# Turning the third weight of the second network in 32 by 32 blocks on VectorE, with four-way loads and a reordered sum

## The chip, the cores and the metric

The kernel runs on one core of one Trainium2 chip. The metric is the time of one execution in microseconds on the device, the median over several runs. Engines are named as in the profile: PE is TensorE (PEld its weight loads), DVE is VectorE, ACT is ScalarE, POOL is GpSimd, SP the engine that here only issues DMAs.

## The reference

Inputs and weights arrive as float64 and are converted on the chip. In short:

```python
attn = concat([a @ state, a2 @ x])       # both softmaxes of x.state^T, 8 batches x 8 heads, 512 + 32 rows, D = 64
x = attn.transpose(0, 2, 1, 3).reshape(8 * 544, 512)
h = np.maximum(x @ w_in, 0.0)            # w_in 512 x 2048   first network
x = h * h @ w_out                        # w_out 2048 x 512
a = x @ w1                               # 512 x 1024        second network
b = x @ w2
h = a * b @ w3                           # w3 1024 x 1024    "third weight"
return h @ w_out2                        # w_out2 1024 x 512
```

No nonlinearity stands between `w3` and the second network's `w_out`, which the kernel calls `w_out2`. The kernel multiplies these two weights with each other once.

## The kernel before

The batches are called c = 0 to 7, with a short ninth group of rows behind them. For each c the first network runs over f = 0 to 15: `h_tile(c, f)` makes 128 of the 2048 hidden columns with six matmuls (L456, tiles `ph`), ACT takes relu and square (L442, L444), and the result is split into a high and a low part of fp32r (`split`: a cast on ACT, L84, and a subtraction on DVE, L85; tile `ghl`). `y_tile(c, f)` follows two tiles behind and adds that slice times `w_out` to the four output banks with twelve matmuls (L494, three passes over high and low parts, `PASSES`). The weight `sw` that `h_tile` reads holds the product of a group of four f with the state: eight small matmuls (L426, `ps_sw`), split again by a cast and a subtraction.

Between these tiles lies the attention of the next batch. `load_xb` loads x in 16 small transfers (L247), `turn_x` turns it in 32 by 32 blocks on DVE (L257, tiles `xT`), eight small matmuls make the scores (L295, `ps_s`), ACT copies them out (L301, tiles `S`), and DVE and ACT do the softmax (L306 to L340). `ps_s`, `ps_sw` and a few others share one PSUM tag, `bank_m`, with two buffers, so `ps_sw` can be written only when ACT has copied the scores out.

Also between the tiles, about one piece for every second tile, the weights of the second network are converted from float64 ("later" pieces 0 to 39: `w_out2`, then 16 of `w3`, then `w1` and `w2`). `load_later` loads one piece of 128 partitions x 512 numbers in a 512 KB transfer (tag `raw`, three buffers, which the x transfers share). `exponents` and `convert64` turn it into float32 with five DVE instructions (L128, L146, L149, L152, L155) and one on ACT (L129). `make_later` stores it from tile `cw` to a scratch in DRAM (L214). All loads and stores are issued by SP, in order.

When the first network ends, w3 comes back from the scratch (`load_stage`, L641, tiles `wst`, a row block kk of 128 x 1024 each). `w3_xpose(kk)` turns it on PE with eight transposes of 128 x 128 (L692, two halves of four, into `bank_m`), and splits each half from PSUM into `w3T`. `w34_rows(kk)` multiplies it with `w_out2` in 24 matmuls (L707). There are eight row blocks. The transposes of the next block stand ahead of the matmuls of this one. Then the second network's products (`quad`, L822, and `out_tile`, L903) run to the end.

The order of instructions on each engine is not the order of the program: the framework's scheduler places instructions of the parts that run beside each other, with gates between some tiles. A change in one part can therefore move the others on every queue. The functions touched, and what calls them:

Of the kernel before, what the change touches and what calls it, by code (L numbers as in the profile page):

```python
# [8 lines left out]
F32 = mybir.dt.float32  # L9
F32R = mybir.dt.float32r  # L10
# [10 lines left out]
def kernel(  # L21
# [37 lines left out]
    def f32(ap):  # L59
        return ap.bitcast(F32)  # L60
# [10 lines left out]
    def bank_m(name):  # L71
        return psum.tile([P, 512], F32, tag="m", bufs=2, name=name)
# [7 lines left out]
    def split(hi, lo, src, hi_on_vector=False):  # L80
        if hi_on_vector:
            nc.vector.tensor_copy(hi, src)
        else:
            nc.scalar.copy(hi, src)  # L84
        return nc.vector.tensor_tensor(out=lo, in0=src, in1=f32(hi), op=ALU.subtract)  # L85
# [20 lines left out]
    def raw_tile(early, name="raw"):  # L106

        if early:
            return wpool.tile([P, 512, 2], I32, tag="wo", bufs=NF, name=name)
        return att.tile([P, 512, 2], I32, tag="raw", bufs=3, name=name)  # L110

    def load64(key, src, early=False):

        t = raw_tile(early)
        flat = t.rearrange("p a b -> p (a b)")
        if isinstance(src, list):
            n = 1024 // len(src)
            for i, a in enumerate(src):
                nc.sync.dma_start(flat[:, i * n:(i + 1) * n], a.bitcast(I32))
        else:  # L120
            nc.sync.dma_start(flat, src.bitcast(I32))
        raws[key] = t
# [9 lines left out]
    def convert64(key, out):  # L132


        t = raws.pop(key)
        hw, lw = t[:, :, 1], t[:, :, 0].bitcast(U32)
        if len(out.shape) == 3:
            n = out.shape[2]
            hw, lw = (v.rearrange("p (k n) -> p k n", n=n) for v in (hw, lw))
        if key not in exps:  # L140
            exponents(key, t)
        e = exps.pop(key)
        m = att.tile([P, 512], I32, tag="cm", bufs=1, name="cm")
        if len(out.shape) == 3:
            e, m = (v.rearrange("p (k n) -> p k n", n=n) for v in (e, m))
        nc.vector.tensor_scalar(  # L146
            out=m, in0=hw, scalar1=0xFFFFF, scalar2=0x100000, op0=ALU.bitwise_and, op1=ALU.bitwise_or
        )
        nc.vector.scalar_tensor_tensor(  # L149
            out=f32(m), in0=lw, scalar=2.0**-32, in1=m, op0=ALU.mult, op1=ALU.add  # L150
        )
        nc.vector.scalar_tensor_tensor(  # L152
            out=e, in0=hw, scalar=-(2**31), in1=e, op0=ALU.bitwise_and, op1=ALU.bitwise_or
        )
        nc.vector.scalar_tensor_tensor(  # L155
            out=out, in0=f32(m), scalar=2.0**-20, in1=f32(e), op0=ALU.mult, op1=ALU.mult
        )

    def load_win(fg, k):
        load64(("win", fg, k), w_in[k * P:(k + 1) * P, fg * 512:(fg + 1) * 512])  # L160
# [33 lines left out]

        open_splits.append(halves)

    w3_s = [dram.tile([P, 2, 512], F32, name=f"w3s{i}") for i in range(N1)]
    w12_s = [[dram.tile([P, 2, 512], F32, name=f"w12s{i}_{k}") for k in range(ND)] for i in range(2)]
    wo2_s = [dram.tile([P, 2, 512], F32, name=f"wo2s{i}") for i in range(N1 // 2)]
    later = [(wo2_s[j // 2][:, j % 2, :], w_out2[j * P:(j + 1) * P, :]) for j in range(N1)]  # L200
    for src, dst in ((w3, w3_s), (w1, w12_s[0]), (w2, w12_s[1])):
        later += [
            (dst[k][:, h, :], src[k * P:(k + 1) * P, h * 512:(h + 1) * 512])
            for k in range(src.shape[0] // P) for h in range(2)
        ]

    def load_later(i):
        if i < len(later):
            load64(("later", i), later[i][1])

    def make_later(i):
        w = att.tile([P, 512], F32, tag="cw", bufs=1, name="cw")
        convert64(("later", i), w)
        nc.sync.dma_start(later[i][0], w)  # L214

    stT = att.tile([P, B, HG, NS], F32, name="stT")
    x9T = pa.tile([P, ND, NT9], F32, tag="x9", name="x9T")
# [421 lines left out]
    def load_stage(key, src):  # L639
        t = w34p.tile([P, 2, 512], F32, tag="wst2", bufs=4, name="wst2")  # L640
        nc.sync.dma_start(t, src)  # L641
        stage[key] = t

    def load_wo2(i):
        load_stage(("wo2", i), wo2_s[i])

    def split_wo2(j):
        t = w34p.tile([P, 2, DM], F32R, tag="wo2", bufs=N1, name="wo2")
# [1 line left out]
        wo2_t[j] = t  # L650

    def load_w3(kk):
        load_stage(("w3", kk), w3_s[kk])

    order = [(c, f) for f0 in (0, 4) for c in range(2) for f in range(f0, f0 + 4)]
    order += [(2, f) for f in range(8)] + [(c, f) for c in range(3) for f in range(8, NF)]
# [28 lines left out]

    w3T = {}

    def w3_xpose(kk):
        for half in range(2):
            ps = bank_m("ps_w3")  # L690
            for j in range(4):
                nc.tensor.transpose(  # L692
                    ps[:, j * P:(j + 1) * P], stage["w3", kk][:, half, j * P:(j + 1) * P], ident
                )
            t = pa.tile([P, 2, 512], F32R, tag=f"sw{half}", bufs=2, name="w3T")
            split(t[:, HI], t[:, LO], ps)
            w3T[kk, half] = t

    w34_t = {}
    w34_s = [dram.tile([P, 2, 2, DM], F32, name=f"w34s{i}") for i in range(N1 // 4)]  # L700
# [221 lines left out]


    rows = list(range(N1 // 2, N1)) + list(range(N1 // 2))
    w3_xpose(rows[0])
    while pend:
        y_tile(*pend.pop(0))
    raw = load_w(0)
    for i, kk in enumerate(rows):
        if i + 1 < N1:  # L930
            w3_xpose(rows[i + 1])
        if i + 4 < N1:
            load_w3(rows[i + 4])
        w34_rows(kk)
        if i == 3:
            make_w(raw)
# [71 lines left out]
```

## Time and profile before

| | us |
|---|---|
| median of 3 runs | 1257.79 |
| the 3 runs | 1257.40, 1257.79, 1259.08 |
| profiled execution | 1257.84 |
| its span | 1256.1 |

Mean granted clock of PE over the span: 0.999 of full speed. 1.74 us of the profiled execution lie outside its span. The page of the profile gives the busy time of each engine, the chain of waits that ended last, and groups of instructions by line. The timeline of an engine gives when each group of equal instructions started and for how long it was busy, with the idle time before it; since matmuls are pipelined, the next one starts before the last one has ended, and the distance of two starts is what a matmul costs on PE.

### The profile page before, as it was taken

Reading aid. Unit: us, or ns where it says so; the run is one execution under the profiler, and the core shown is the slowest. Engines: PE = TensorE matmul, PEld = TensorE weight load, DVE = VectorE, ACT = ScalarE, POOL = GpSimd, SP = SyncE. Lnnn points to the kernel's source line nnn. Section 1 sums busy time; section 2 is a strip of 40 time slices with the busy share of each in tenths; the row PEclk is TensorE's granted clock in tenths of the full one; section 3 lists DMA queues with packets and bytes.
Section 4 is the critical chain, followed back from the end, with each engine's and each line's share of the span. In section 5 each row is a group of like instructions: output and inputs, shape, how many; then the busy total and the mean of one; then the engine's idle time right before and its main releaser. Section 6 shows DMA issues by size and latency. Waiting matters only on the chain.

```text
span 1256.1 us, 17499 instructions
## 1 busy us (share of the span) xinstructions
PE 1235.1 (98%) x6672; PEld 982.1 (78%) x6672; DVE 789.0 (63%) x1403; ACT 659.3 (52%) x1188; POOL 33.5 (3%) x30
## 2 busy tenths in 40 slices
PE   6999999999999999999999999999999999999998
PEld 4667777777777777777799888888888888887886
DVE  6998778677585867742435835555655647474753
ACT  5687768666575756645655434444443524242430
POOL 0000000000000000000000000001500010000000
PEclk9999999999999999999999999999999999999999
DMA  6264646462634535201313520313430521423213
GB/s 218 69 207 145 173 129 201 113 184 82 156 130 86 190 76 173 89 18 34 134 42 111 201 76 9 120 48 126 143 134 9 201 76 52 149 74 128 76 59 117
DMA packets 125268, 143.23 MB, mean 114 GB/s; under 512 B 71680, under 2 KB 75264, under 8 KB 124672
## 3 DMA queue, kind: packets, MB, share of 16 engines
q1 hardware_dynamic: 125184, 142.11, 36.5%
q8 instruction: 52, 0.85, 0.3%
q14 instruction: 32, 0.26, 0.1%
HBM read 96.47 MB, written 45.61 MB: 113 GB/s over the span
## 4 chain that ended last, share of the span: by engine, by line
PE 93%; DMA 2%; ACT 2%; DVE 2%; issue 1%; SPq 0%; ACTq 0%; DVEq 0%
PE y L494 29%; PE po L903 14%; PE qa L822 10%; PE qd L822 7%; PE qc L822 3%; PE ps_w L707 3%; PE qe L822 3%; PE ps_sw L426 3%; PE ab L877 2%; DMA x<-in_x_dram 1%; PE ps_w L692 1%; PE ps_a L364 1%; PE ps_r L372 0%; PE ps_s L295 0%; DMA out_dram<-o 0%
## 5 line engine op out<-in xcount | busy, mean ns | idle before, releaser
L494 PE MATMUL y<-ghl,wo 128*128 128x512 f32 (+1 forms) x1728 | 403.0, 381 | 0.6 <-ACT wo L84 0.5
L494 PEld LDWEIGHTS y<-ghl,wo 128*128 128x128 f32 x1728 | 309.1, 188 | 88.4 <-ACT r L442 12.6
L85 DVE TENSOR_TENSOR ghl<-r,ghl 128x512 fp32r<-128x512 f32 (+1 forms) x144 | 95.0, 660 | 170.1 <-ACT ghl L84 167.4
L822 PE MATMUL qa<-yq,wq 128*128 128x512 f32 x576 | 146.3, 390 | 1.4 <-ACT s L830 1.4
L830 ACT COPY s<-qa 128x512 f32<-128x512 f32 x96 | 56.2, 589 | 143.7 <-PE qa L822 131.2
L822 PEld LDWEIGHTS qa<-yq,wq 128*128 128x128 f32 x576 | 107.5, 188 | 25.5 <-ACT s L830 2.4
L822 PE MATMUL qd<-yq,wq 128*128 128x512 f32 x384 | 98.4, 390 | 0.0
L903 PE MATMUL po<-w34b,c 128*128 128x512 f32 x408 | 95.8, 391 | 0.3 <-DVE o L912 0.3
L903 PE MATMUL po<-w,c 128*128 128x512 f32 x408 | 95.5, 391 | 0.0
L903 PEld LDWEIGHTS po<-w34b,c 128*128 128x128 f32 x408 | 75.7, 188 | 18.0 <-DVE c L85 1.0
L903 PEld LDWEIGHTS po<-w,c 128*128 128x128 f32 x408 | 75.5, 188 | 17.7 <-ACT o L909 1.1
L444 ACT ACTIVATE r<-r 128x512 f32<-128x512 f32 (+1 forms) x144 | 87.5, 608 | 2.9
L84 ACT CAST ghl<-r 128x512 fp32r<-128x512 f32 (+1 forms) x144 | 86.0, 597 | 3.5
L822 PEld LDWEIGHTS qd<-yq,wq 128*128 128x128 f32 x384 | 71.8, 188 | 15.7 <-ACT s L830 0.9
L129 ACT ACTIVATE ce<-ce,ebias 128x512 int32<-128x512 int32 x72 | 52.3, 727 | 44.3 <-DVE ce L128 44.3
L834 DVE TENSOR_TENSOR s<-qa,s 128x512 f32<-128x512 f32 x32 | 22.1, 692 | 75.0 <-ACT s L830 75.0
L780 POOL TENSOR_TENSOR yraw<-yraw,yp 128x512 f32<-128x512 f32 x24 | 32.8, 1373 | 987.9 <-DMA yraw<-yscr 815.2
L84 ACT CAST c<-s 128x512 fp32r<-128x512 f32 x64 | 39.7, 622 | 37.1 <-DVE s L851 36.1
L84 ACT CAST yq<-yraw 128x512 fp32r<-128x512 f32 x70 | 42.6, 622 | 24.1 <-DVE yraw L797 15.5
L912 DVE TENSOR_TENSOR o<-po,opart 128x512 f32<-128x512 f32 x34 | 23.3, 689 | 47.1 <-PE po L903 37.6
L152 DVE SCALAR_TENSOR_TENSOR ce<-raw,ce 128x512 int32<-128x512 int32 x72 | 49.3, 685 | 1.7 <-ACT ce L129 1.7
L85 DVE TENSOR_TENSOR yq<-yraw,yq 128x512 fp32r<-128x512 f32 x70 | 46.8, 684 | 5.0 <-ACT yq L84 4.7
(551 smaller groups left out, 1806.6 us busy)
## 6 DMA issues: line engine op xcount, KB each, us to landing
raw<-in_moe_w_dram SPq DMA_DIRECT2D x32, 512.0 KB, 4.3
yraw<-yscr SPq DMA_DIRECT2D x56, 256.0 KB, 5.5
yscr<-yo SPq DMA_DIRECT2D x52, 256.0 KB, 2.6
raw<-in_moe_w_out_dram SPq DMA_DIRECT2D x24, 512.0 KB, 3.9
oscr<-o SPq DMA_DIRECT2D x34, 256.0 KB, 2.2
opart<-oscr SPq DMA_DIRECT2D x34, 256.0 KB, 2.9
out_dram<-o SPq DMA_DIRECT2D x32, 256.0 KB, 2.9
raw<-in_moe_w_in_dram SPq DMA_DIRECT2D x12, 512.0 KB, 3.9
```

What stands on the lines that cost most here:

```text
L84: nc.scalar.copy(hi, src)
L85: return nc.vector.tensor_tensor(out=lo, in0=src, in1=f32(hi), op=ALU.subtract)
L129: nc.scalar.activation(e, e, ACTF.Relu, bias=ebias, scale=8.0)
L152: nc.vector.scalar_tensor_tensor(out=e, in0=hw, scalar=-(2**31), in1=e, op0=ALU.bitwise_and, op1=ALU.bitwise_or)
L426: mm = nc.tensor.matmul(pss[r][k * NS:(k + 1) * NS, cols], stT[rows, b, k, :], win_t[fg][rows, k, cols], start=True, stop=True, tile_posit ...
L444: nc.scalar.activation(r[:, :n], r[:, :n], ACTF.Square)
L494: nc.tensor.matmul(y_ps[c, d][:, :n], wo_t[f][:, wi, d * P:(d + 1) * P], t[:, gi, :n], start=(f == f0 and k == 0), stop=(f == f1 - 1 and k ...
L707: nc.tensor.matmul(ps, t[:, wi, (j % 4) * P:(j % 4 + 1) * P], wo2_t[j][:, vi, :], start=(j == 0 and k == 0), stop=(j == N1 - 1 and k == 2),)
L780: nc.gpsimd.tensor_tensor(out=t[:, n], in0=t[:, n], in1=p, op=ALU.add)
L822: nc.tensor.matmul(ps, W[w, kt][:, wi, m * P:(m + 1) * P], Y[v, kt][:, vi, :], start=(first and kt == 0 and k == 0), stop=(last and kt == ...
L830: nc.scalar.copy(t, ps)
L903: nc.tensor.matmul(ps, v[:, vi, t * P:(t + 1) * P], w[:, wi, :], start=(m == 0 and k == 0), stop=(m == QM - 1 and k == 2),)
```

## The change

The 16 pieces of w3 get another shape and another way. A piece is now 64 rows x 1024 columns. It is loaded by four transfers: each brings 256 columns of the 64 rows to one quarter (32) of the partitions. The conversion ends in the tile `cm` in place of `cw`, and one DVE instruction turns its 128 x 512 numbers in 32 by 32 blocks into `cw`, which is stored. The scratch is one DRAM tile. When it is read back, block by block, partition 32a+q of the part with number k holds column 256a+32k+q of w3, so the sum over w3's columns runs in another order, and `w_out2` is loaded in that order too, by four transfers of 32 partitions in place of one. The eight transposes on PE per row block are gone; the split reads the loaded tile in SBUF through a view whose innermost run is 32 numbers. Number and shapes of the product's matmuls (L707, now L729) stay as they are.

```diff
--- before.py
+++ after.py
@@ -134,14 +134,14 @@
 
         t = raws.pop(key)
         hw, lw = t[:, :, 1], t[:, :, 0].bitcast(U32)
-        if len(out.shape) == 3:
+        if out is not None and len(out.shape) == 3:
             n = out.shape[2]
             hw, lw = (v.rearrange("p (k n) -> p k n", n=n) for v in (hw, lw))
         if key not in exps:
             exponents(key, t)
         e = exps.pop(key)
         m = att.tile([P, 512], I32, tag="cm", bufs=1, name="cm")
-        if len(out.shape) == 3:
+        if out is not None and len(out.shape) == 3:
             e, m = (v.rearrange("p (k n) -> p k n", n=n) for v in (e, m))
         nc.vector.tensor_scalar(
             out=m, in0=hw, scalar1=0xFFFFF, scalar2=0x100000, op0=ALU.bitwise_and, op1=ALU.bitwise_or
@@ -153,8 +153,9 @@
             out=e, in0=hw, scalar=-(2**31), in1=e, op0=ALU.bitwise_and, op1=ALU.bitwise_or
         )
         nc.vector.scalar_tensor_tensor(
-            out=out, in0=f32(m), scalar=2.0**-20, in1=f32(e), op0=ALU.mult, op1=ALU.mult
+            out=f32(m) if out is None else out, in0=f32(m), scalar=2.0**-20, in1=f32(e), op0=ALU.mult, op1=ALU.mult
         )
+        return f32(m)
 
     def load_win(fg, k):
         load64(("win", fg, k), w_in[k * P:(k + 1) * P, fg * 512:(fg + 1) * 512])
@@ -194,24 +195,46 @@
 
         open_splits.append(halves)
 
-    w3_s = [dram.tile([P, 2, 512], F32, name=f"w3s{i}") for i in range(N1)]
+    w3_s = dram.tile([P, 4 * N1, 256], F32, name="w3s")
     w12_s = [[dram.tile([P, 2, 512], F32, name=f"w12s{i}_{k}") for k in range(ND)] for i in range(2)]
-    wo2_s = [dram.tile([P, 2, 512], F32, name=f"wo2s{i}") for i in range(N1 // 2)]
-    later = [(wo2_s[j // 2][:, j % 2, :], w_out2[j * P:(j + 1) * P, :]) for j in range(N1)]
-    for src, dst in ((w3, w3_s), (w1, w12_s[0]), (w2, w12_s[1])):
+    wo2_s = dram.tile([D1, DM], F32, name="wo2s")
+    later = [(wo2_s[j * P:(j + 1) * P, :], w_out2[j * P:(j + 1) * P, :]) for j in range(N1)]
+    w3_v = w3.rearrange("(i d q) (a c) -> i a q d c", d=2, q=NS, a=4)
+    later += [(w3_s[:, 2 * i:2 * i + 2], [w3_v[i, a] for a in range(4)]) for i in range(2 * N1)]
+    for src, dst in ((w1, w12_s[0]), (w2, w12_s[1])):
         later += [
             (dst[k][:, h, :], src[k * P:(k + 1) * P, h * 512:(h + 1) * 512])
             for k in range(src.shape[0] // P) for h in range(2)
         ]
 
+    turned = range(N1, N1 + 2 * N1)
+
     def load_later(i):
-        if i < len(later):
+        if i >= len(later):
+            return
+        if i >= turned.stop:
             load64(("later", i), later[i][1])
+            return
+        t = raw_tile(False)
+        flat = t.rearrange("p a b -> p (a b)")
+        if i in turned:
+            for q, a in enumerate(later[i][1]):
+                nc.sync.dma_start(
+                    flat[q * NS:(q + 1) * NS].rearrange("p (d c) -> p d c", d=2), a.bitcast(I32)
+                )
+        else:
+            nc.sync.dma_start(flat, later[i][1].bitcast(I32))
+        raws["later", i] = t
 
     def make_later(i):
-        w = att.tile([P, 512], F32, tag="cw", bufs=1, name="cw")
-        convert64(("later", i), w)
-        nc.sync.dma_start(later[i][0], w)
+        if i in turned:
+            m = convert64(("later", i), None)
+            w = att.tile([P, 512], F32, tag="cw", bufs=1, name="cw")
+            nc.vector.transpose(out=w, in_=m)
+        else:
+            w = att.tile([P, 512], F32, tag="cw", bufs=1, name="cw")
+            convert64(("later", i), w)
+        nc.sync.dma_start(later[i][0], w.rearrange("p (d c) -> p d c", d=2) if i in turned else w)
 
     stT = att.tile([P, B, HG, NS], F32, name="stT")
     x9T = pa.tile([P, ND, NT9], F32, tag="x9", name="x9T")
@@ -642,7 +665,10 @@
         stage[key] = t
 
     def load_wo2(i):
-        load_stage(("wo2", i), wo2_s[i])
+        t = stage["wo2", i] = w34p.tile([P, 2, 512], F32, tag="wst2", bufs=4, name="wst2")
+        rows = wo2_s.rearrange("(a k p) e -> a p k e", a=4, p=NS)
+        for a in range(4):
+            nc.sync.dma_start(t[a * NS:(a + 1) * NS], rows[a, :, 2 * i:2 * i + 2, :])
 
     def split_wo2(j):
         t = w34p.tile([P, 2, DM], F32R, tag="wo2", bufs=N1, name="wo2")
@@ -650,7 +676,7 @@
         wo2_t[j] = t
 
     def load_w3(kk):
-        load_stage(("w3", kk), w3_s[kk])
+        load_stage(("w3", kk), w3_s[:, 4 * kk:4 * kk + 4].rearrange("p (h d) c -> p h (d c)", h=2))
 
     order = [(c, f) for f0 in (0, 4) for c in range(2) for f in range(f0, f0 + 4)]
     order += [(2, f) for f in range(8)] + [(c, f) for c in range(3) for f in range(8, NF)]
@@ -685,16 +711,12 @@
 
     w3T = {}
 
-    def w3_xpose(kk):
+    def w3_split(kk):
+        src = stage["w3", kk].rearrange("p h (d k q) -> p k (h d) q", d=2, q=NS)
         for half in range(2):
-            ps = bank_m("ps_w3")
-            for j in range(4):
-                nc.tensor.transpose(
-                    ps[:, j * P:(j + 1) * P], stage["w3", kk][:, half, j * P:(j + 1) * P], ident
-                )
-            t = pa.tile([P, 2, 512], F32R, tag=f"sw{half}", bufs=2, name="w3T")
-            split(t[:, HI], t[:, LO], ps)
-            w3T[kk, half] = t
+            t = pa.tile([P, 2, 4, 4, NS], F32R, tag=f"sw{half}", bufs=2, name="w3T")
+            split(t[:, HI], t[:, LO], src[:, 4 * half:4 * half + 4])
+            w3T[kk, half] = t.rearrange("p s k d q -> p s (k d q)")
 
     w34_t = {}
     w34_s = [dram.tile([P, 2, 2, DM], F32, name=f"w34s{i}") for i in range(N1 // 4)]
@@ -922,13 +944,13 @@
 
 
     rows = list(range(N1 // 2, N1)) + list(range(N1 // 2))
-    w3_xpose(rows[0])
+    w3_split(rows[0])
     while pend:
         y_tile(*pend.pop(0))
     raw = load_w(0)
     for i, kk in enumerate(rows):
         if i + 1 < N1:
-            w3_xpose(rows[i + 1])
+            w3_split(rows[i + 1])
         if i + 4 < N1:
             load_w3(rows[i + 4])
         w34_rows(kk)
```

The instructions that the scheduler places stand as follows in the two programs. Names: `ps_s` are scores, `ps_sw` the bank of the state product, `ph_n` an h tile of f = n, `y_` an output bank of the first network, `sw_` the split state product, numbers behind a name count tiles.

PE in batch c = 5 before: where the scores of the next batch (`ps_s`), the state product for f = 4 to 7 (`ps_sw`) and the tiles around them stand.

```order
L295 MATMUL ps_s<-xT,stT 32x512 x8
L456 MATMUL ph_1__4358<-aT_3910,sw_4223 128x512 x3
L456 MATMUL ph_1__4358<-aT_4128,sw_4226 128x512 x3
L426 MATMUL ps_sw<-win_710,stT 32x512 x8
L494 MATMUL y_3714<-ghl,wo_2131 128x512 x3
L494 MATMUL y_3715<-ghl,wo_2131 128x512 x3
L494 MATMUL y_3716<-ghl,wo_2131 128x512 x3
L494 MATMUL y_3717<-ghl,wo_2131 128x512 x3
L456 MATMUL ph_2__4411<-aT_3910,sw_4223 128x512 x3
L456 MATMUL ph_2__4411<-aT_4128,sw_4226 128x512 x3
```

PE in batch c = 5 now, at the same place.

```order
L517 MATMUL y_4490<-ghl,wo_694 128x512 x3
L517 MATMUL y_4491<-ghl,wo_694 128x512 x3
L517 MATMUL y_4492<-ghl,wo_694 128x512 x3
L517 MATMUL y_4493<-ghl,wo_694 128x512 x2
L318 MATMUL ps_s<-xT,stT 32x512 x2
L517 MATMUL y_4493<-ghl,wo_694 128x512
L318 MATMUL ps_s<-xT,stT 32x512 x2
L449 MATMUL ps_sw<-win_700,stT 32x512 x8
L479 MATMUL ph_4__4547<-aT_3957,sw_4435 128x512
L479 MATMUL ph_5__4601<-aT_3957,sw_4435 128x512
L479 MATMUL ph_4__4547<-aT_3957,sw_4435 128x512 x2
L479 MATMUL ph_4__4547<-aT_4180,sw_4438 128x512 x3
```

The scores and the state product stood behind f = 0 and 1, with an h tile between them and y tiles behind; now they stand behind f = 3, next to each other, and the next tile is the first that reads the new product `sw_4435`. The first four of the eight score matmuls now stand ahead of the h tile of f = 3.

DVE in batch c = 5 before: from the first instruction on the scores to the subtractions that complete `sw`.

```order
L306 TENSOR_REDUCE nm<-S 128x1
L321 STREAM_TRANSPOSE e_4463<-S 128x512
L308 TENSOR_SCALAR nm_4454<-nm 128x1
L329 TENSOR_REDUCE mx<-e_4463 128x16
L330 TENSOR_TENSOR e_4463<-e_4463,mx 128x512
L313 TENSOR_SCALAR rs<-sm 128x1
L314 RECIPROCAL rs<-rs 128x1
L85 TENSOR_TENSOR sw_4381<-ps_sw,sw_4381 128x512
L85 TENSOR_TENSOR ghl<-r,ghl 128x512
L85 TENSOR_TENSOR sw_4384<-ps_sw,sw_4384 128x512
```

DVE in batch c = 5 now, the same stretch, with the new transposition of a piece of w3 (L233) ahead of it.

```order
L233 STREAM_TRANSPOSE cw<-cm 128x512
L329 TENSOR_REDUCE nm<-S 128x1
L146 TENSOR_SCALAR cm<-raw 128x512
L331 TENSOR_SCALAR nm_4508<-nm 128x1
L128 TENSOR_SCALAR ce<-raw 128x512
L149 SCALAR_TENSOR_TENSOR cm<-raw,cm 128x512
L336 TENSOR_SCALAR rs<-sm 128x1
L344 STREAM_TRANSPOSE e_4517<-S 128x512
L155 SCALAR_TENSOR_TENSOR cm<-cm,ce 128x512
L152 SCALAR_TENSOR_TENSOR ce<-raw,ce 128x512
L85 TENSOR_TENSOR sw_4435<-ps_sw,sw_4435 128x512
L85 TENSOR_TENSOR sw_4438<-ps_sw,sw_4438 128x512
```

Instructions of the conversion stand now between the scores and the subtraction for `sw_4435`.

PE in the product of the two weights before, from one row block to the next.

```order
L707 MATMUL ps_w_6902<-wo_6458,w3T 128x512 x3
L707 MATMUL ps_w_6902<-wo_6497,w3T 128x512 x3
L692 MATMUL ps_w_6930<-ident,wst_6461 128x128 x4
L692 MATMUL ps_w_6938<-ident,wst_6461 128x128 x4
L707 MATMUL ps_w_6948<-wo_6216,w3T 128x512 x3
L707 MATMUL ps_w_6948<-wo_6253,w3T 128x512 x3
```

PE there now.

```order
L729 MATMUL ps_w_6948<-wo_6524,w3T 128x512 x3
L729 MATMUL ps_w_6948<-wo_6563,w3T 128x512 x3
L729 MATMUL ps_w_6984<-wo_6282,w3T 128x512 x3
L729 MATMUL ps_w_6984<-wo_6319,w3T 128x512 x3
```

The transposes between the row blocks are gone; nothing stands in their place.

## Rows read from the trace of the kernel before

**Rows 1.** Page, busy time, share of the span and instructions of each engine.

```profile
PE 1235.1 (98%) x6672; PEld 982.1 (78%) x6672; DVE 789.0 (63%) x1403; ACT 659.3 (52%) x1188; POOL 33.5 (3%) x30
```

**Rows 2.** Page, the chain that ended last, shares of the span by line.

```profile
PE y L494 29%; PE po L903 14%; PE qa L822 10%; PE qd L822 7%; PE qc L822 3%; PE ps_w L707 3%; PE qe L822 3%; PE ps_sw L426 3%; PE ab L877 2%; DMA x<-in_x_dram 1%; PE ps_w L692 1%; PE ps_a L364 1%; PE ps_r L372 0%; PE ps_s L295 0%; DMA out_dram<-o 0%
```

**Rows 3.** Windows, one batch each: us, busy of each engine, clock, DMA share, GB/s.

```profile
307.00:382.00 75.00, 74.98 (x447) 56.92 (x446) 52.00 (x99) 46.20 (x81) 0.00 (x0) 1.00 0.48 128
456.00:530.00 74.00, 73.98 (x443) 56.06 (x442) 51.32 (x99) 45.91 (x80) 0.00 (x0) 1.00 0.45 129
```

**Rows 4.** Timeline of PE, the weights' product: start, busy us, line, tiles, count.

```profile
684.75 5.71 PE L707 MATMUL ps_w<-wo,w3T 128*128 128x512 f32 x24
690.30 1.03 PE L692 MATMUL ps_w<-ident,wst 128*128 128x128 f32 x8
691.09 5.70 PE L707 MATMUL ps_w<-wo,w3T 128*128 128x512 f32 x24
...
722.76 11.14 PE L707 MATMUL ps_w<-wo,w3T 128*128 128x512 f32 x48
733.74 2.88 PE L822 MATMUL qa<-yq,wq 128*128 128x512 f32 x12
```

**Rows 5.** Groups by line: instruction, shapes, count, busy us, mean ns, idle before.

```profile
L692 PE MATMUL ps_w<-ident,wst 128*128 128x128 f32 x64 | 8.3, 272 | 0.0
L257 DVE STREAM_TRANSPOSE xT<-xb 128x512 f32<-128x512 f32 x20 | 14.0, 702 | 0.0
L128 DVE TENSOR_SCALAR ce<-raw 128x512 int32<-128x512 int32 x72 | 30.2, 420 | 4.7 <-DMA raw<-in_moe_w_in_dram 2.3 <-DMA raw<-in_moe_w_out_dram 1.8 <-DVE rs L313 0.3
L129 ACT ACTIVATE ce<-ce,ebias 128x512 int32<-128x512 int32 x72 | 52.3, 727 | 44.3 <-DVE ce L128 44.3
L84 ACT CAST w3T<-ps_w 128x512 fp32r<-128x512 f32 x16 | 8.6, 593 | 0.2 <-PE ps_w L692 0.2
L84 ACT CAST wq<-wraw 128x512 fp32r<-128x512 f32 x20 | 11.6, 625 | 5.7 <-DMA wraw<-w12s 5.1 <-DVE wraw L754 0.5
```

**Rows 6.** Timeline of PE in batch c = 4, around the scores of the next.

```profile
341.19 2.88 PE L494 MATMUL y<-ghl,wo 128*128 128x512 f32 x12
344.00 1.09 PE L295 MATMUL ps_s<-xT,stT 64*32 64x512 f32 x16
345.02 1.65 PE L456 MATMUL ph__3636<-aT,sw 128*128 128x512 f32 x6
346.60 1.09 PE L426 MATMUL ps_sw<-win,stT 64*32 64x512 f32 x16
347.62 3.02 PE L494 MATMUL y<-ghl,wo 128*128 128x512 f32 x12
350.48 1.52 PE L456 MATMUL ph__3689<-aT,sw 128*128 128x512 f32 x6
```

**Rows 7.** Timeline of ACT at the same place.

```profile
345.18 1.07 ACT L301 COPY S<-ps_s 128x512 f32<-128x512 f32 x2 [1.41 <-PE ps_s L295]
...
348.48 0.56 ACT L84 CAST sw<-ps_sw 128x512 fp32r<-128x512 f32 x1
```

**Rows 8.** Timeline of DVE at the same place.

```profile
349.07 0.69 DVE L85 TENSOR_TENSOR sw<-ps_sw,sw 128x512 fp32r<-128x512 f32 x1 [0.26 <-ACT sw L84]
349.68 0.68 DVE L85 TENSOR_TENSOR ghl<-r,ghl 128x512 fp32r<-128x512 f32 x1
```

**Rows 9.** Timeline of SP's queue (issue of DMAs) in batch c = 3.

```profile
304.84 13.96 SPq L247 DMA_DIRECT2D xb<-in_x_dram  x16
...
319.43 0.38 SPq L121 DMA_DIRECT2D raw<-in_moe_w_dram  x1
```

**Rows 10.** DMA issues from 100 to 680 us: count, KB each, median us to landing.

```profile
raw<-in_moe_w_dram SPq DMA_DIRECT2D x32, 512.0 KB, 4.3
...
xb<-in_x_dram SPq DMA_DIRECT2D x80, 64.0 KB, 2.3
```

**Rows 11.** Timeline of PE near the start, with the idle time before each group.

```profile
29.45 0.62 PE L426 MATMUL ps_sw<-win,stT 64*32 64x256 f32 x4 [2.62 <-ACT xT L287]
31.16 1.81 PE L426 MATMUL ps_sw<-win,stT 64*32 64x256 f32 x12 [1.08 <-ACT xT L287]
```

**Rows 12.** Windows there, columns as in rows 3: the number behind POOL is the clock.

```profile
32.00:33.00 1.00, 0.97 (x8) 0.09 (x7) 0.57 (x2) 0.00 (x1) 0.00 (x0) 0.50 0.00 0
...
35.00:36.00 1.00, 1.00 (x7) 0.62 (x6) 1.00 (x4) 0.00 (x0) 0.00 (x0) 0.82 0.00 0
```

## The prediction

> **What bounds the kernel now.** I read the page's busy times first: PE is busy 98% of the span [rows 1]. The chain that ended last is PE almost throughout, with the transposes of w3 (L692) at a rounded 1% [rows 2]. The windows then show the stages that the change touches: in a batch of the first network PE works 74.98 of 75 and 73.98 of 74 us, with DVE at 52 and ACT at 46 [rows 3]. PE waits for nothing there. So a microsecond taken from PE's instructions is a microsecond off the end, DVE has some 22 us a batch to spare, and a stall that the change puts into PE is added whole. The profiled execution took 1257.84 us, 0.05 above the median, so the sum can be made against it.
>
> **What is removed.** The timeline of PE shows, in the weights' product, eight transposes and then 24 matmuls, again and again [rows 4]. The eight start at 690.30 and the matmuls behind them at 691.09: 0.79 us. By whole row blocks it is slightly more: with transposes a block takes 691.09 - 684.75 = 6.34 us, the last two, without, take (733.74 - 722.76) / 2 = 5.49 each. The difference is 0.85, and eight blocks give 6.8; by starts it is 8 x 0.79 = 6.3. I take **-6.7 us**. PE never waits in this stage, so all of it counts as long as the split is ready in time.
>
> The groups by line give 272 ns for one transpose [rows 5], but the starts show 0.79 / 8 = 0.1 us each, since they are pipelined. The Trainium skill, "TensorE: Matmul & The Clock Gate", Part 4, gives about 275 ns for a transpose of 128 x 128 in one kernel. That agrees with the row's duration; taken as the cost, 64 x 0.275 us would be a gain of 17.6 us, an estimate from the page that the starts contradict.
>
> **The split from SBUF.** Cast and subtraction stay 16 each. From PSUM the cast takes 593 ns, from SBUF with long runs 625 [rows 5]; runs of 32 numbers are not shown. The nearest row with blocks of 32 is the block transposition, 702 ns for 128 x 512 [rows 5]. Between 0.6 and 0.7 us each the split takes at most 2 x 0.1 us longer per half and has a row block of 5.5 us for two halves. I take zero on PE. If such runs cost double, 2 x 0.65 us per half, 2.6 per block, it still fits the block; the bound is +1 us for the first.
>
> **The turning on DVE.** Sixteen instructions, 702 ns each by the row of the turned x [rows 5], make 11.2 us, about 0.7 in every second tile. DVE's spare 22 us a batch [rows 3] hides the amount. It does not hide the order, and this is the main point.
>
> **The loads.** 48 more issues for w3, 12 more for w_out2, all on SP. One issue costs 0.38 us alone; a run of 16 of x took 13.96, 0.87 each [rows 9], as only so many are outstanding. A piece's four thus take 1.5 to 3.5 us in place of 0.4. Landing is bounded by 64 KB in 2.3 us and 512 KB in 4.3 [rows 10]. The x transfers queue behind them and share the three `raw` buffers, so the scheduler turns x later on DVE, and the scores on PE move too.
>
> The Trainium skill, "Perfetto Trace Analysis", section "What DMA-bound means", says that where the issuing engine's queue is solid with transfers, large descriptors are what matters, which speaks against four small loads. SP's row of 13.96 us is such a stretch, but PE waits for none of it here; by the page the loads would be a loss, by the windows nothing.
>
> **Moved order, c = 5.** Before, an h tile lies between scores and `ps_sw`, and a y tile and an h tile behind: PE goes 344.00, 345.02, 346.60, 347.62, 350.48 without a gap (batch c = 4 in the trace, the same pattern) [rows 6]. Meanwhile ACT copies the scores from 345.18 and casts the first `sw` at 348.48 [rows 7]; DVE's subtraction runs from 349.07 to 349.76 [rows 8]. From the end of the scores (345.02) to a complete `sw` are 4.7 us, all of it under the cover of 1.6 us of h and 2.9 of y and more.
>
> In the new order the y tiles are used up first. Behind the last two scores come `ps_sw` at once, and then the h tile of f = 4, which reads the new `sw`. Only `ps_sw` (1.02) and two matmuls (0.45) lie within the chain. With the old chain the exposed part is 4.7 - 1.02 - 0.45 = 3.2 us. But the new chain is longer: between the exponential and the cast ACT now has L129 (727 ns busy [rows 5]), and DVE has L146, L128, L149, the block transposition of `e`, L155 and L152 ahead of the subtraction. I laid both queues out by hand at 0.60 us a start, as DVE's rows 349.07 and 349.68 show [rows 8], and 0.36 for the shorter kind (L128 and L146, 420 ns busy [rows 5]). With the scores ending at 0: copies 0.15 to 1.2, maximum to 1.3, exponential 2.0 to 2.8, L129 to 3.35, first cast to 3.85; DVE's subtraction 4.9 to 5.6. Stall: 5.6 - 1.5 = **+4.2** (range 3.2 to 5).
>
> Then DVE is behind. From that subtraction to the one for `ghl` of f = 5 stand 16 long instructions, 6 shorter and some tiny ones: 16 x 0.60 + 6 x 0.36 + 0.5 = 12.3, end at 5.6 + 12.3 + 0.2. PE has, at a matmul of 0.227 us (24 in 5.49 [rows 4]), ten matmuls of f = 4 and 5, the next `ps_sw` 1.0, three tiles of 1.36, 2.72 and 1.36, and nine matmuls: 10.8 us. Stall **+1.6** (0 to 3), and about **+0.4** for the y tiles near it.
>
> **Moved order, c = 4 and 6.** The scores are broken in two by y and h tiles there. In c = 4 the last scores wait for an `xT` behind a copy of y on DVE, one or two DVE instructions of 0.6; in c = 6 `ps_sw` follows two y matmuls behind the last scores, while the copies need 0.15 + 1.07 [rows 7]. I take **+0.6** and **+0.8**, each 0 to 1.5. From there to the weights' product PE's order is the old one.
>
> **The sum.** -6.7 + 0 (split) + 4.2 + 1.6 + 0.4 + 0.6 + 0.8 = +0.9. 1257.84 + 0.9 = 1258.7 us.
>
> **The rivals.** *The stalls as laid out* (the sum): 1258.7, with all bounds of the stalls from 3.2 + 0 + 0 + 0 to 5 + 3 + 0.4 + 1.5 + 1.5, so 1254.3 to 1262.5. For it speaks that PE, ACT and DVE work in order; against it, that the layout is by hand.
>
> *The clock falls* (slower). Near the start PE idled 2.62 us and, after 0.62 of work, 1.08 [rows 11]; behind this the granted clock was 0.50, the 1.2 GHz level, for three windows of 1 us, the first of which is shown, and 0.82 in the last [rows 12]. That is 3 x 0.5 + 0.18 = 1.7 us lost. The idle stretch in c = 5 is as long in sum (4.2) with short work in it. If the clock falls there, 1258.7 + 1.7 = 1260.4; after the second stall again, 1262. It decides from a stall near 4 us; against it speaks that PE had been full before and that the stall is broken up. The Trainium skill, "TensorE: Matmul & The Clock Gate", Part 1, has the half rate as what idleness leads to, and sustained work as what ends it; the rows agree.
>
> *The moved order costs little* (faster). If ACT and DVE run ahead of my layout, or the copies and the cast overlap so that y tiles still cover them, the gain stands almost whole: 1257.84 - 6.7 + 1 = 1252, and 1251.1 with no stall. Against it stands that before, the same chain took 4.7 us with less on DVE.
>
> *The four loads are late* (slower). A piece has two tiles, 2 x (1.36 + 2.72) = 8.2 us, to be loaded; issue at 0.87 x 4 = 3.5 and landing at 4.3 sum to 7.8. Past 8.2 us DVE's L128 waits in order with `ghl` behind it. Half a microsecond for 10 of the 16 pieces reaching PE is 5 us: 1264. Y tiles two behind speak against it.
>
> *The transposes cost their 272 ns* (faster): -17.4 + 7.6 = 1248.0; the starts rule it out nearly.
>
> **How the numbers follow.** Chances: stalls as laid out 0.42; clock falls 0.30; little cost 0.18; loads late 0.09; full 272 ns 0.01. About 0.2%, 2.5 us, is what a measurement of this kernel tells from no change: below 1255.3 is faster, above 1260.3 slower. The first case has 0.03 below, 0.34 inside, 0.05 above; the second 0.13 inside, 0.17 above; the third 0.14 below, 0.04 inside; the fourth 0.01 inside, 0.08 above; the fifth is below. Faster 0.18, same 0.52, slower 0.30. Since the first two sit close together, the range from 1253.5 to 1262.5 leaves out most of the third case and of the fourth, under 0.2.
>
> **What would show it.** No transposes in the product, row blocks of 5.49 us and qa some 6.7 us nearer to the first block: the gain. In c = 5 a gap of PE before the first tile that reads the new `sw`, released by ACT's cast or DVE's subtraction, and a second before the last y matmuls of f = 5. Granted clock under 1 behind it for the second case. Waits of DVE for the raw w3 tile would show the fourth. I am wrong if PE stays at 74 of 74 in c = 4 to 6, or if the product's row blocks wait for the split.

## The result and the profile after

The changed kernel takes 1267.28 us in the median of six runs (1265.99 to 1268.45), the kernel before 1257.94 beside it. The ratio is 1.0071, with a 95% interval from 1.0060 to 1.0081: slower by 9.3 us, where 1258.7 and a range up to 1262.5 had been forecast. The profiled execution took 1266.46, its span is 1264.7, 8.6 more than before.

The page's busy times and the chain that ended last, after (they answer to [rows 1] and [rows 2]):

```profile
PE 1235.4 (98%) x6608; PEld 976.0 (77%) x6608; DVE 799.0 (63%) x1419; ACT 659.0 (52%) x1188; POOL 32.7 (3%) x30
...
PE 82%; DVE 7%; DMA 5%; ACT 3%; issue 1%; SPq 1%; DVEq 0%; ACTq 0%
```

PE has 64 instructions fewer and the same busy time, and only 82% of the chain. Before, the chain by engine read:

```profile
PE 93%; DMA 2%; ACT 2%; DVE 2%; issue 1%; SPq 0%; ACTq 0%; DVEq 0%
```

The gain itself is there. This is the timeline of PE in the weights' product, which answers to [rows 4]:

```profile
697.37 43.71 PE L729 MATMUL ps_w<-wo,w3T 128*128 128x512 f32 x192
740.91 2.88 PE L844 MATMUL qa<-yq,wq 128*128 128x512 f32 x12
```

Eight row blocks run in 740.91 - 697.37 = 43.5 us, 5.44 each, without a gap. To see where time was lost before them, the starts of the first h tile of each batch were read from the two timelines of PE:

| start of | before | after | difference | change in the stretch that ends there |
|---|---|---|---|---|
| c = 3 | 265.69 | 266.08 | +0.39 | |
| c = 4 | 339.83 | 340.00 | +0.17 | -0.2 |
| c = 5 | 413.96 | 416.64 | +2.68 | +2.5 |
| c = 6 | 488.09 | 499.04 | +10.95 | +8.3 |
| c = 7 | 562.23 | 576.50 | +14.27 | +3.3 |
| ninth group | 631.29 | 645.56 | +14.27 | 0.0 |
| first qa | 733.74 | 740.91 | +7.17 | -7.1 |
| end of the span | 1256.1 | 1264.7 | +8.6 | +1.4 |

So the product gives 7.1 us back, and c = 4, 5 and 6 cost 14.1. The waits of PE between 100 and 690 us, where before there were none:

```profile
PE ph__4547 L479 <- ACT sw L84: 1.5, 1, 1.5
PE y L517 <- DVE ghl L85: 1.5, 2, 1.1
PE ps_a L387 <- DVE sw L85: 1.1, 1, 1.1
PE ph__4547 L479 <- DVE sw L85: 0.8, 1, 0.8
PE ps_sw L449 <- ACT S L324: 0.7, 1, 0.7
PE y L517 <- ACT yo L527: 0.5, 1, 0.5
PE ps_r L395 <- DVE sw L85: 0.2, 1, 0.2
```

They add up to 6.3 us, of which 0.5 (the copy `yo`) lies before c = 3. So 5.8 of the 14.1 us in c = 4 to 6 are waits, and the larger part, 8.3, lies where PE counts as busy. The timeline of PE in c = 5 shows both parts:

```profile
427.15 1.06 PE L318 MATMUL ps_s<-xT,stT 64*32 64x512 f32 x8
...
439.49 1.05 PE L318 MATMUL ps_s<-xT,stT 64*32 64x512 f32 x4
440.47 0.50 PE L517 MATMUL y<-ghl,wo 128*128 128x512 f32 x1
440.90 1.05 PE L318 MATMUL ps_s<-xT,stT 64*32 64x512 f32 x4
442.62 1.57 PE L449 MATMUL ps_sw<-win,stT 64*32 64x512 f32 x16 [0.67 <-ACT S L324]
445.73 0.50 PE L479 MATMUL ph__4547<-aT,sw 128*128 128x512 f32 x1 [1.53 <-ACT sw L84]
446.06 0.40 PE L479 MATMUL ph__4601<-aT,sw 128*128 128x512 f32 x1
447.23 1.43 PE L479 MATMUL ph__4547<-aT,sw 128*128 128x512 f32 x5 [0.77 <-DVE sw L85]
...
459.61 0.96 PE L517 MATMUL y<-ghl,wo 128*128 128x512 f32 x3 [1.08 <-DVE ghl L85]
```

The waits are those of the forecast: on the copies, on the cast, on the subtraction, and a second one on the `ghl` of f = 5. What was not forecast is the cost of the split scores. (The eight score matmuls of a batch stand in the timeline as 16 records, two for each.) A group of four records takes from 439.49 to 440.47, 0.98 us, though [rows 6] has 16 of them in 1.02. The groups by line of the kernel before had said so:

```profile
L295 PE MATMUL ps_s<-xT,stT 64*32 64x512 f32 x128 | 10.4, 658 | 0.7 <-ACT stT L526 0.7
```

One record lasts 658 ns in the mean, and 16 together 1.02 us: they run beside each other. A separate group of four or of eight records takes nearly as long again as all 16.

### The profile page after: what moved, and what is told of

The parts are those of the page before. It is cut to its first block, busy times and chain, and to the rows that moved or that the text cites. A ratio compares the mean times of both kernels' runs of the same rounds, so it can differ in the third digit from the quotient of the medians.

```text
span 1264.7 us, 17477 instructions
## 1 busy us (share of the span) xinstructions
PE 1235.4 (98%) x6608; PEld 976.0 (77%) x6608; DVE 799.0 (63%) x1419; ACT 659.0 (52%) x1188; POOL 32.7 (3%) x30
## 4 chain that ended last, share of the span: by engine, by line
PE 82%; DVE 7%; DMA 5%; ACT 3%; issue 1%; SPq 1%; DVEq 0%; ACTq 0%
PE y L517 26%; PE po L925 11%; PE qa L844 10%; PE qd L844 6%; PE ps_w L729 3%; PE qc L844 3%; PE qe L844 3%; PE ps_sw L449 2%; PE ab L899 2%; DVE yq L85 1%; DMA x<-in_x_dram 1%; DMA yraw<-yscr 1%; PE ps_s L318 1%; DMA raw<-in_moe_w_out_dram 1%; DMA w12s<-cw 1%
## 5 line engine op out<-in xcount | busy, mean ns | idle before, releaser
L149 DVE SCALAR_TENSOR_TENSOR cm<-raw,cm 128x512 f32<-128x512 uint32 x72 | 49.2, 683 | 0.4
```

Of the source, the lines that this page charges most:

```text
L149: nc.vector.scalar_tensor_tensor(out=f32(m), in0=lw, scalar=2.0**-32, in1=m, op0=ALU.mult, op1=ALU.add)
```

## Experiments

**Theory A**: the four loads of a piece make the scheduler set another order in c = 4 to 6, and the order costs, by waits and by groups of scores that are split. **Theory B**: the 16 block transpositions crowd DVE. **Theory C**: the four loads themselves are late or block SP. The expectations say which order each variant has.

**The four loads alone.** In the kernel before:

```diff
+        elif key[0] == "later" and N1 <= key[1] < 3 * N1:
+            for q in range(4):
+                nc.sync.dma_start(flat[q * NS:(q + 1) * NS].rearrange("p (d c) -> p d c", d=2), src[q * NS:(q + 1) * NS].rearrange("p (d c) -> p d c", d=2).bitcast(I32))
```

> The kernel before, with one edit: each of the 16 pieces of w3 is loaded by four transfers of 32 partitions in 2 KB runs; PE transposes w3 as before and DVE turns nothing of it. Its order on PE is that of the changed kernel: the scores of c = 4, 5 and 6 stand in three, three and two groups. Theory A (the four loads move the order, and the order costs): the whole loss of the changed kernel without its gain of 7.1 us, so 1258 + 14 to 16 = 1272 to 1274 us. Theory B (the 16 block transpositions crowd DVE, and that costs): near 1258 us.

Measured: 1272.17 us, before 1258.62 beside it, ratio 1.0106 (1.0091 to 1.0121). No piece is turned on DVE and nothing is missing on PE, and the loss is 13.6 us. PE's timeline has the scores in the same pieces:

```profile
438.46 1.05 PE L298 MATMUL ps_s<-xT,stT 64*32 64x512 f32 x4
439.87 1.05 PE L298 MATMUL ps_s<-xT,stT 64*32 64x512 f32 x4
```

Theory B falls as the main cause. But unlike in the changed kernel's profile, the clock fell here in c = 5. PE waited 0.67 and 1.53 us at the same two places, and the windows behind (columns as in [rows 3]) show the lower level:

```profile
445.00:446.00 1.00, 1.00 (x3) 0.57 (x3) 1.00 (x2) 0.13 (x1) 0.00 (x0) 0.50 0.90 352
447.00:448.00 1.00, 1.00 (x4) 0.77 (x3) 1.00 (x3) 0.02 (x1) 0.00 (x0) 0.50 0.00 0
```

With 0.88 in the window from 444 and 0.92 in that from 448, 1.7 us are lost to it. By its trace this run loses 13.3 us in c = 4 to 6: 3.8 in waits, 1.7 by the clock and 7.8 elsewhere, where the changed kernel has 8.3.

**One load, still turned.** In the changed kernel:

```diff
-            for q, a in enumerate(later[i][1]):
-                nc.sync.dma_start(
-                    flat[q * NS:(q + 1) * NS].rearrange("p (d c) -> p d c", d=2), a.bitcast(I32)
-                )
+            nc.sync.dma_start(flat, w3[(i - N1) // 2 * P:(i - N1) // 2 * P + P, (i - N1) % 2 * 512:(i - N1) % 2 * 512 + 512].bitcast(I32))
```

> The changed kernel, with each piece of w3 loaded by one transfer of 128 rows x 512 columns; the elements then lie in other places, so w3 enters the product shuffled, with the same number and shape of every other instruction. The scores stand in one group in every batch again. Theory A (order): only the gain is left, 1258 - 7 = 1251 us. Theory B (the block transpositions on DVE): the loss stays, 1265 to 1267 us.

Measured: 1252.12 us, ratio 0.9945 (0.9930 to 0.9960), 6.5 us faster than before. Between 100 and 690 us PE waits 0.0 us. The scores of the next batch stand whole in c = 5, as in [rows 6]:

```profile
419.09 1.09 PE L315 MATMUL ps_s<-xT,stT 64*32 64x512 f32 x16
420.11 1.65 PE L476 MATMUL ph__4364<-aT,sw 128*128 128x512 f32 x6
421.69 1.09 PE L446 MATMUL ps_sw<-win,stT 64*32 64x512 f32 x16
```

The turning on DVE and the split from SBUF cost nothing that can be seen.

**x four tiles earlier.** In the changed kernel:

```diff
-            side[i - 4].append(lambda b=b, g=g: load_xb(b, g))
-            side[i - 2].append(lambda b=b, g=g: turn_x(b, g))
+            side[i - 8].append(lambda b=b, g=g: load_xb(b, g))
+            side[i - 6].append(lambda b=b, g=g: turn_x(b, g))
```

> The changed kernel, complete, with the transfers of x and its turning on DVE written four tiles earlier in the program; four loads per piece and 16 block transpositions stay. The scores stand in one group in every batch again. Theory A (order): 1251 us. Theory C (the four loads themselves are late or block SP, whatever the order): the loss stays, 1264 to 1268 us. Theory B: the same as C.

Measured: 1257.80 us, ratio 0.9992 (0.9982 to 1.0001), between the two. The loss of 9.3 us is gone (now -0.8), but 5.7 remain against the run with one load. From c = 3 to c = 7 PE loses 5.0 us instead of 13.9. The scores are whole; PE's waits now name others:

```profile
PE y L517 <- DVE yo L525: 1.1, 2, 0.7
PE ps_a L387 <- DVE sw L85: 1.1, 2, 0.8
PE ps_sw L449 <- ACT S L324: 0.9, 2, 0.6
PE ps_a L387 <- DVE rs L336: 0.5, 1, 0.5
PE y L517 <- ACT yo L527: 0.4, 1, 0.4
```

They sum to 4.0 us. On DVE's timeline, two copies of y stand among conversions of the weights, back to back:

```profile
432.26 0.68 DVE L155 SCALAR_TENSOR_TENSOR cm<-cm,ce 128x512 f32<-128x512 f32 x1
432.86 0.68 DVE L525 COPY yo<-y 128x512 f32<-128x512 f32 x1
433.46 0.70 DVE L233 STREAM_TRANSPOSE cw<-cm 128x512 f32<-128x512 f32 x1
434.09 0.39 DVE L128 TENSOR_SCALAR ce<-raw 128x512 int32<-128x512 int32 x1
434.39 0.42 DVE L146 TENSOR_SCALAR cm<-raw 128x512 int32<-128x512 int32 x1
434.72 0.68 DVE L525 COPY yo<-y 128x512 f32<-128x512 f32 x1
```

DVE's order differs from that of the run with one load, and PE waits for what stands late in it. Between 240 and 640 us DVE waits for no load here, but four times for a store out of `cw`, 0.3 to 2.3 us. Theory A covers this only if the order on DVE counts as well as that on PE; theory C was not excluded yet.

**Scores in two groups.** In the kernel before, `scores` makes the first four matmuls of the batches 4 to 7 and a second function, one tile later, the other four:

```diff
-            for k in range(HG):
+            for k in range(HG // 2 if b > BLK else HG):
...
-                [sc], [], [s2[0], s1a[0]], [],
+                [sc], [sc_], [s2[0], s1a[0]], [],
```

> The kernel before, with the eight score matmuls of each of the batches b = 4 to 7 written in two groups of four, one tile apart; nothing is added or removed. If a group costs by its matmuls, as the prediction took it, PE does the same work and the time stays within 1 us of 1258. If a group of four takes as long as one of eight, about 1.0 us, as the changed kernel's timeline suggests, four more groups cost 4 us: 1262 us, and 1 to 2 us more where PE then waits for the state product.

Measured: 1264.41 us, ratio 1.0046 (1.0028 to 1.0065): 5.8 us for four groups more. PE waits for nothing in c = 3 to 6, and loses 1.5 us in each:

```profile
270.02 1.06 PE L305 MATMUL ps_s<-xT,stT 64*32 64x512 f32 x8
271.01 1.65 PE L468 MATMUL ph__2906<-aT,sw 128*128 128x512 f32 x6
...
275.33 1.06 PE L305 MATMUL ps_s<-xT,stT 64*32 64x512 f32 x8
276.32 0.96 PE L468 MATMUL ph__2967<-aT,sw 128*128 128x512 f32 x3
277.21 1.45 PE L438 MATMUL ps_sw<-win,stT 64*32 64x512 f32 x16
278.59 0.97 PE L468 MATMUL ph__2967<-aT,sw 128*128 128x512 f32 x3
```

Each half takes 0.99 us, nearly as the whole did (1.02). Of the rest, some 0.5 us, 0.36 lies at `ps_sw`, which now breaks an h tile and takes 1.38 from start to start in place of 1.02.

**Scores whole.** In the changed kernel:

```diff
-            for k in range(HG):
+            for k in reversed(range(HG)):
```

> The changed kernel, complete, with the score matmuls of a batch written from the last part of x to the first, so that they wait for the last turned x and stand in one group in every batch; in c = 4, 5 and 6 that group stands right ahead of the state product, with nothing between. If a separate group costs about 1 us whatever its size, five groups fewer (two in c = 4, two in c = 5, one of 0.7 us in c = 6) give 4.7 us; the state product then waits 0.7 us for the copies in c = 4 and 6 in exchange, and the stalls behind the scores of c = 5 stay: 1267 - 4.7 + 1.4 = 1264 us. If groups cost nothing, 1267 or more.

Measured: 1262.55 us, ratio 1.0027 (1.0016 to 1.0037), with 1258.92 for before. Against before, the loss falls from 9.3 to 3.6 us: 5.7, where 3.3 had been worked out. Joining the groups thus takes off about a third of the 16 us that stand against the gain (9.3 + 7.1). The order around the scores moves with them, and the profiled execution, 1265.38 us, was longer than the median, so its trace is read by parts: c = 4 to 6 lose 10.4 us, 6.7 of it in waits and 1.7 by the clock, which fell behind one wait of 1.90 us (granted 0.50 from 531 to 533 us). Only 2.0 lie elsewhere, where the changed kernel has 8.3: 6.3 less for five groups fewer.

**Not turned.** In the changed kernel, `convert64` writes `cw` and the transposition is left out:

```diff
-            m = convert64(("later", i), None)
             w = att.tile([P, 512], F32, tag="cw", bufs=1, name="cw")
-            nc.vector.transpose(out=w, in_=m)
+            convert64(("later", i), w)
```

> The changed kernel without the 16 block transpositions on DVE, so that w3 enters the product with its 32 by 32 blocks not turned; the four loads stay, all on SP, and the scores of c = 4, 5 and 6 stand in groups as in the changed kernel. Theory A: 1265 to 1267 us, within 2 us of the changed kernel. Theory B (DVE's transpositions cost): 1251 to 1256.

Measured: 1264.85 us, ratio 1.0043 (1.0030 to 1.0057). Without a transposition on DVE 5.9 us of loss remain, against 9.3 with them. In this order the turning carries up to 3.4 us, 1 us or 2 more than theory A had said, although it cost nothing in the run with one load. By the traces, c = 4 to 6 lose 12.8 us here and 14.1 in the changed kernel; the difference is in the waits, 4.6 against 5.8. So 1.3 of the 3.4 us are seen where the order moved; the rest is not located.

**Loads by two engines.** In the changed kernel:

```diff
-            for q, a in enumerate(later[i][1]):
-                nc.sync.dma_start(
+            for q, (a, dma) in enumerate(zip(later[i][1], (nc.sync, nc.sync, nc.gpsimd, nc.gpsimd))):
+                dma.dma_start(
```

> The changed kernel, complete, with two of the four loads of each piece issued by SP and two by GpSimd. The same transfers, bytes and block transpositions; PE's instructions stand in the order of the kernel before, without the transposes, and DVE's nearly so. Theory A (the order alone costs): 1251 to 1252 us, like the run with one load. If what remained in the run with x four tiles earlier (6 us above the run with one load) came from the four transfers themselves, 1256 to 1258.

Measured: 1253.44 us, ratio 0.9958 (0.9946 to 0.9971), 5.5 us faster than before with the whole computation. The transfers are the same 64; only who issues half of them, and by this the order, has changed. 1253.44 lies 1.4 us above theory A's range and 2.6 below the other: most of the loss is gone, and between 100 and 690 us PE still waits 0.7, 0.6 and 0.4 us. Theory C falls in the form that the four transfers are late by themselves. That four issues block SP is not excluded by this run alone, since SP has only half of them here. This is the fastest complete version by its median, and it beats both kernels.

**Three or four by GpSimd, and two by SP.** The same edit with one load by SP and three by GpSimd, then with all four by GpSimd; then, all by SP, two transfers of 64 partitions:

```diff
-            for q, a in enumerate(later[i][1]):
-                nc.sync.dma_start(
-                    flat[q * NS:(q + 1) * NS].rearrange("p (d c) -> p d c", d=2), a.bitcast(I32)
-                )
+            for q in range(2):
+                nc.sync.dma_start(flat[q * 64:(q + 1) * 64], w3[(i - N1) // 2 * P + q * 64:(i - N1) // 2 * P + q * 64 + 64, (i - N1) % 2 * 512:(i - N1) % 2 * 512 + 512].bitcast(I32))
```

> The changed kernel, complete, with one of the four loads of each piece issued by SP and three by GpSimd. PE's order is that of the kernel before without the transposes, and DVE's stands as near to it as in the run with one load. Theory A (order): 1251 to 1253 us, as that run. If GpSimd's share of the issues costs by itself, since four loads by it took 1260: between 1253 and 1260.

> The changed kernel, complete, with all four loads of each piece issued by GpSimd. PE's order is that of the kernel before without the transposes; 60 of DVE's conversion instructions more than in the run with two stand elsewhere. Theory A: 1251 to 1253 us. If the issuing engine matters by itself (GpSimd shares a path with VectorE, or its issues take longer), 1254 or more.

> The changed kernel with each piece loaded by two transfers of 64 partitions, both issued by SP; as in the run with one load, the elements lie in other places and w3 enters the product shuffled. The order on PE is that of the kernel before without the transposes, and DVE's as in the run with two loads by GpSimd. Theory A: 1252 to 1254 us, as that run, whichever engine issues.

Measured: 1254.98 with three (ratio 0.9970, 0.9958 to 0.9982), 1253.87 with two by SP (0.9962, 0.9950 to 0.9975), but 1260.43 with four by GpSimd (1.0010, 1.0001 to 1.0019). Two transfers by SP lie in theory A's range. Three by GpSimd do not: 1254.98 is above 1251 to 1253 and in the range expected if GpSimd's share costs by itself. Four, at 1260.43, are a clear miss of theory A ("1254 or more" was the other branch): the order on PE is that of the kernel before, yet in c = 4 the run loses 6.1 us in one place. On PE's timeline the state product waits there for the copies of the scores:

```profile
353.81 2.44 PE L449 MATMUL ps_sw<-win,stT 64*32 64x512 f32 x16 [3.11 <-ACT S L324]
```

That is half of the 6.1. Most of the other 3.0 us is the clock, which fell in this wait to the lower level, until 359.5 us:

```profile
354.00:355.00 1.00, 1.00 (x9) 0.22 (x14) 1.00 (x3) 0.45 (x2) 0.87 (x2) 0.50 0.79 252
358.00:359.00 1.00, 1.00 (x4) 0.75 (x3) 1.00 (x2) 1.00 (x3) 0.00 (x0) 0.50 0.00 0
```

The run with three loads by GpSimd has a wait at the same place, 3.3 us lost, and keeps its clock at 1.00:

```profile
349.64 1.57 PE L449 MATMUL ps_sw<-win,stT 64*32 64x512 f32 x16 [2.48 <-ACT S L324]
```

In the run with four, on DVE's timeline, a little earlier, the transposition waits for a store:

```profile
349.70 0.71 DVE L233 STREAM_TRANSPOSE cw<-cm 128x512 f32<-128x512 f32 x1 [5.72 <-DMA w3s<-cw]
```

The transposition writes the single `cw` buffer, which is free only when the piece before has been stored; the median store of this line lands after 3.1 us in that trace, the longest after 9.0. Around it GpSimd issued twelve loads of w3 from 336 to 345 us, and these landed after 2.8 to 8.8 us, 7.5 in the median, where the 64 loads of the changed kernel took 3.2. With three loads by GpSimd the store at this place landed after 7.2. So loads and stores were slow together; that it comes from more loads under way at once is likely, but no run changes that alone. This is a real wait on a transfer, which the order alone doesn't tell, and GpSimd's issues bring it: theory A doesn't cover it.

## Why the prediction was wrong

**The gain** was right: -6.7 forecast, -7.1 in the product. Turning on DVE took 699 ns each (702 forecast), and the cast from SBUF in runs of 32 took 618 ns, inside the bounds; no row block waited:

```profile
L233 DVE STREAM_TRANSPOSE cw<-cm 128x512 f32<-128x512 f32 x16 | 11.2, 699 | 0.0
L84 ACT CAST w3T<-wst 128x512 fp32r<-128x512 f32 x16 | 9.9, 618 | 2.5 <-issue 1.7 <-PE ps_w L729 0.6 <-ACT yq L84 0.2
```

That PE's transposes cost their pitch of 0.1 us and not the 272 ns of one was right too.

**The waits in c = 5** were about right. Forecast were 4.2 for the chain, 1.6 and 0.4; the timeline has 0.67 + 1.53 + 0.77 = 3.0 for the chain and 1.08 + 0.45 + 0.22 = 1.8 behind it. (By its own terms the first is 5.6 - 1.5 = 4.1, not 4.2, and the second 12.3 + 0.2 - 10.8 = 1.7, not 1.6; the two slips cancel.) The hand layout was too long for the subtraction: DVE reached it at 446.49, 4.6 us after the scores' end at 441.88, where 4.9 had been laid out. In c = 4 PE waited for nothing, where 0.6 had been laid out; in c = 6 it waited 1.1 us, near the 0.8, but at `ps_a` for a subtraction, not at `ps_sw` for the copies.

**The step that failed** is "Moved order, c = 5" together with "c = 4 and 6": the split scores were costed by their waits alone, 0 in c = 5 and 0.6 and 0.8 in the others, as if a group cost by its matmuls. By rows, a group of four records takes 0.98 us and one of twelve 1.68, while all 16 took 1.02. In c = 4 the groups take 0.99 + 0.98 + 0.98 in place of 1.02, +1.9; in c = 5 1.00 + 0.98 + 0.98, +1.9; in c = 6 1.68 + 0.98, +1.6. `ps_sw`, behind a broken tile or a wait, adds 0.3 to 0.5 in each. That makes 6.6 us of the 8.3 that no wait explains. The run with the scores in two shows it apart from the loads (+5.8 us for four groups more), and the one with the scores whole shows the 8.3 go down to 2.0. The remaining 1.7 us, probably at h and y tiles that are broken in pieces, were not measured by themselves. By the sum: forecast for c = 4 to 6 was +7.6, measured +14.1.

The Trainium skill, "TensorE: Matmul & The Clock Gate", Part 3, gives the span of small matmuls at different tile positions as the duration of one plus a few nanoseconds for each further one. The rows agree that a group's time hardly depends on how many stand in it: two or four matmuls (four or eight records) take 0.98 to 1.0 us, eight take 1.02. They differ in the level, 0.98 against the 658 ns of one record, as the two records of a matmul start 0.45 us apart in the trace. By rows alone the prediction could have put at least 0.66 us, the length of one record, on each of the five extra groups: 3.3 us, an estimate, which it had at nothing.

**The clock** didn't fall in the profiled execution. The forecast gave this case 0.30; in c = 5 the granted clock stays full in the worst stretch (windows, columns as in [rows 3]):

```profile
444.00:445.00 1.00, 0.20 (x7) 0.00 (x0) 0.99 (x4) 1.00 (x3) 0.00 (x0) 1.00 0.00 0
445.00:446.00 1.00, 0.27 (x1) 0.28 (x2) 1.00 (x3) 1.00 (x3) 0.00 (x0) 1.00 0.30 74
446.00:447.00 1.00, 0.46 (x2) 0.02 (x1) 1.00 (x2) 0.16 (x1) 0.00 (x0) 1.00 0.94 365
```

The length of the stall doesn't tell it, against the forecast's "from a stall near 4 us". In the run with the four loads alone the clock fell with waits of 0.67 and 1.53 us at the same two places, and cost the 1.7 us of the forecast's second case; with the scores whole it fell behind one of 1.90. It stayed at 1.00 here, with 0.77 more, and through 2.48 us in one piece with three loads by GpSimd. What decides it stays open, and for the other executions of the changed kernel only the mean clock is on record, 0.994 to 0.997.

**The loads** were not late by themselves in the changed kernel: the 64 transfers of 128 KB land after 3.2 us, and four take 1.8 to 2.0 us of SP's queue for twelve of the 16 pieces, near the lower bound of 1.5, and 2.7 to 3.9 for the others. Between 240 and 640 us DVE waits for DMA only twice, 0.79 and 0.52 us, both times for a store and never for a load. The upper bound of 3.5 came from a misreading: [rows 9]'s run of 16 is not solid. Its eighth issue ends at 308.89 and its ninth starts at 314.65, and the wait between them ended with an instruction of DVE, not with a transfer; a single issue of x takes 0.49 us in the median, not 0.87. The forecast had seen that they move the x transfers; the traces show by how much. The transfers of x for c = 4, 5 and 6 begin at 315.06, 404.82 and 478.10 in SP's timeline, 304.84, 378.96 and 453.10 before.

**Left open.** 1.4 us of the span lie behind the first qa; 0.9 of them are waits of PE on ACT's copies (2.3 in place of 1.4), the rest is within what runs of one kernel differ by. Why, in the order with four loads, the turning costs up to 3.4 us was not taken apart further, and the 5.7 us that remain with x four tiles earlier are put down to DVE's order by argument only.

## What to carry to other kernels

Where a scheduler sets the order, compare the order of the changed kernel on the bounding engine first, and cost every group of small matmuls that it splits as one more full group, not as the same work. A load split into several issues can cost far more through the order that it brings than through its transfers: here one extra issue pattern cost 14 us, and giving half of it to another queue brought the order, and 5.5 of the 7.1 us of the gain, back. If a change is meant to take work from the bounding engine, measure its parts in an order that stays, as the run with one load does; then mend the order.

## What was not expected of the hardware

- Eight score matmuls, 64x512 on 64 by 32 tiles, 16 records, take 1.02 us together; four take 0.99, two 0.98. Four extra groups cost 5.8 us of a run.
- Three waits of PE that sum to 3.0 us within 5.3 us (441.9 to 447.2) left the granted clock at 1.00, where in another run 0.67 and 1.53 us at the same places were followed by 0.50. A single wait of 1.90 us was followed by 0.50, one of 2.48 by 1.00, and one of 3.11 by 0.50 for six windows of 1 us.
- With all four loads issued by GpSimd, a store through SP took up to 9.0 us to land and held DVE for 5.72; twelve loads around it took 7.5 in the median, against 3.2 when SP issued them.
